# Delta-rule attention: operands of 128 columns for the products with the state and with the solved values

## The chip, the cores and the metric

The kernel runs on one core of one Trainium2 chip. The core has five engines that run side by side, each with its own row of instructions in a fixed order: TensorE (PE, the matrix products), VectorE (DVE), ScalarE (ACT), GpSimd (POOL) and SyncE (SP, which here only issues DMAs). They wait for each other by semaphores. TensorE writes its products into PSUM, which this program cuts into eight banks of 512 fp32 numbers for each of the 128 partitions; DVE and ACT read them there. The metric is the device time of one execution in microseconds (us).

## The reference

Two stages run one after the other: a delta-rule attention over 768 tokens (4 batches, 8 heads, head size 48), and a feed-forward net with a squared ReLU over the 3072 rows that come out of it.

```python
def _attn_ref(q, k, v, beta):
    B, H, S, D = q.shape                                   # 4, 8, 768, 48
    k_n = k / (np.linalg.norm(k, axis=-1, keepdims=True) + 1e-06)
    state = np.zeros((B, H, D, D), dtype=np.float32)
    y = np.zeros_like(q)
    for t in range(S):
        kt, vt, bt = (k_n[:, :, t], v[:, :, t], beta[:, :, t, None])
        y[:, :, t] = np.einsum('bhd,bhde->bhe', q[:, :, t], state)
        v_old = np.einsum('bhde,bhd->bhe', state, kt)
        state = state + bt[:, :, :, None] * np.einsum('bhd,bhe->bhde', kt, vt - v_old)
    return y

def _moe_ref(x, w_in, w_out):                              # (3072, 384), (384, 2048), (2048, 384)
    h = np.maximum(x @ w_in, 0.0)
    return h * h @ w_out
```

## The kernel before

**Chunks.** The tokens are cut into 12 units of 64 (`units`, `C`). Within a unit the recurrence is solved as a triangular system: with the scores of keys against keys masked below the diagonal, the values corrected by what the state at the unit's start already holds (keys times state) are multiplied by the inverse of that system (`solved`, L549); then the state gets keys times solved values, and the output is queries times old state plus masked query-key scores times solved values. All 32 pairs of batch and head of a unit are treated together: 64 tokens lie on half of the 128 partitions, batches b and b + 2 side by side as `c`, the heads as four pairs p of an even and an odd one (j).

**Steps of a unit.**
- `load`, `load_q`: keys go by DMA into one of three tiles `kpad`, queries into `qpad`, each head padded from 48 to 64 columns with zeros that L90 and L93 have put there at the program's start. `normalize` (L285 to L298) divides the keys by their norms.
- `static`: keys and queries are transposed on TensorE, one head pair per instruction (L335), copied from PSUM by ACT (L338, tile `kq`), multiplied to key-key and key-query scores (L351), which DVE masks (L361, tile `ap`). The first two units do this in two halves, keys first and queries later, with copies on ACT and the mask on POOL. The key-key scores go out to DRAM and come back in another layout (`lt`).
- `invert`: DVE inverts diagonal blocks of 32 x 32 column by column (L448, L449; for the first two units together L446 and L449). The result goes through DRAM into `tt`.
- `whole`: the off-diagonal blocks by two sets of 32 x 32 products (L490, L500; DVE transposes one operand, L483; ACT copies the result to `tt`, L506). Between them stand the products with the old state, two sets of 64 x 48 outputs (L525): keys first, into two banks of pool x, which DVE subtracts from the values (L533), then queries, into two banks of pool g, where they stay.
- `solved`, then `onward`: keys times solved values (L565) into two x banks, which DVE adds to `state`; masked scores times solved values (L574) on top of what stands in the g banks; ACT copies the sum out as `y` (L578).
- `moe` of the unit: y is transposed (L591) and split into a high and a low fp32r part, and the two products with the weights run as three terms each (L625 into an h bank, Relu, Square and split on ACT and DVE at L632 to L635 and L604, and L612 into the o banks).

The feed-forward weights are split at the start and during unit 1 in the same manner (L138 to L163).

**PSUM.** Pools g, x, h and o have two banks each. Tiles of a pool are given out in turn: who wants a bank waits until its last reader is done.

**What sets the order.** Each engine's order is written out by hand: the program lists pieces of work (generators), and `weave` merges them by places between 0 and 1 in a unit. `CHAIN` gives the four places of `whole` (two parts), `solved` and `onward` among 32 steps of the feed-forward of the unit before. While the state part of unit u runs, the feed-forward of unit u - 1 fills TensorE.

Of the kernel before, what the change touches and what calls it, by code (L numbers as in the profile page):

```python
# [21 lines left out]
def kernel(  # L22
# [42 lines left out]
    ps_x = ctx.enter_context(tc.tile_pool(name="ps_x", bufs=2, space=bass.MemoryType.PSUM))  # L65
# [15 lines left out]
    mask = const.tile([P, 2, C], F32, name="mask")  # L81
    nc.gpsimd.memset(mask, 1.0)
    for b in range(2):
        half = mask[b * C:(b + 1) * C, 1]
        nc.gpsimd.affine_select(out=half, in_=half, pattern=[[1, C]], base=0, channel_multiplier=-1,
                                compare_op=ALU.is_gt, fill=0.0)
    kpad = []
    for i in range(3):
        kp = const.tile([P, NC, H, C], F32, name=f"kpad{i}")
        nc.gpsimd.memset(kp[:, :, :, D:], 0.0)  # L90
        kpad.append(kp)
    qp = const.tile([P, NC, H, C], F32, name="qpad")
    nc.gpsimd.memset(qp[:, :, :, D:], 0.0)  # L93
# [132 lines left out]
    def split_bank():  # L226

        turn[1] += 1
        return (ps_o.tile([P, PC], F32, name=f"o{turn[1] % 2}") if split_early else ps_x.tile([P, PC], F32, name="x"))
# [7 lines left out]
    def load_to(dst, x, d, width, queues=None):  # L237
# [6 lines left out]
        for j, queue in enumerate(queues or (nc.sync, nc.sync)):  # L244
            for b, src in enumerate(tokens(x, d)):
                rows = slice((b ^ j) * C, (b ^ j) * C + C)
                for c in range(NC):
                    queue.dma_start(out=dst[rows, c, j::2, :width], in_=src[:, c, j::2])

    def load(u):  # L250
        d = dict(u=u, y=[None] * NC)
        d["kp"] = kpad[u % 3]
        load_to(d["kp"], k, d, D, (nc.sync, nc.scalar) if u <= 1 else None)
        return d

    def load_q(d):

        d["qp"] = kpad[2] if d["u"] == 1 else qp
        load_to(d["qp"], q, d, D)
# [13 lines left out]
    def load_v(d):  # L273
        d["vt"] = apool.tile([P, NC, H, D], F32, name="vt", bufs=2)
        load_to(d["vt"], v, d, D)

    def normalize(d):

        n2, s0, s1 = [apool.tile([P, H2], F32, name=f"{n}{d['u'] % 2}", bufs=1) for n in ("n2", "s0", "s1")]
        kn = d["kp"].rearrange("p c h d -> p (c h) d")[:, :, :D]  # L280
        squares = []
        for c in range(NC):
            sq = (apool.tile([P, H, D], F32, name="r", bufs=2) if d["u"] in (2, 3) else
                  spool.tile([P, PC], F32, name="rest")[:, :H * D].rearrange("p (h e) -> p h e", h=H))
            nc.scalar.activation(out=sq, in_=kn[:, c * H:(c + 1) * H], func=AF.Square)  # L285
            squares.append(sq)
        yield
        for c, sq in enumerate(squares):
            nc.vector.tensor_reduce(out=n2[:, c * H:(c + 1) * H], in_=sq, axis=AX.X, op=ALU.add)  # L289
# [11 lines left out]
        nc.vector.tensor_tensor(out=kn, in0=kn, in1=s1.unsqueeze(2).broadcast_to(list(kn.shape)), op=ALU.mult)  # L301
        yield

    def x_tile(u=2):

        turn[0] += 1
        pool, name = (ps_h, "h") if u <= 1 and turn[0] % 4 >= 2 else (ps_x, "x")
        return pool.tile([P, PC], F32, name=name)


    def static(d):

        u = d["u"]
        room = dram.tile([4, H2, HB, HB], F32, name="blocks")

        kq = apool.tile([P, NC, NP, 2, 2, C], F32, name="kq", bufs=2)
        ap = apool.tile([P, NC, H, 2, C], F32, name="ap", bufs=2)
        d["kq"], d["ap"] = kq, ap


        def banks(c):
            if c == 0 or u <= 1:
                return [x_tile(u) for _ in range(2)]
            g = ps_g.tile([P, 2, PC], F32, name="g")
            return [g[:, 0], g[:, 1]]

        def transposed(parts, pair, into):

            pair = [x.rearrange("p (x n t) -> p x n t", x=2, n=NP) for x in pair]
            for x, (c, which) in enumerate(parts):  # L330
                src = d["qp" if which else "kp"]
                for p in range(NP):
                    for b in range(2):
                        rows = slice(b * C, (b + 1) * C)
                        nc.tensor.transpose(pair[b][:, x, p], src[rows, c, 2 * p:2 * p + 2].rearrange("p a b -> p (a b)"),  # L335
                                            ident[rows, rows])
            for b in range(2):
                nc.scalar.copy(out=into[:, :, :, b], in_=pair[b])  # L338

        def products(c, first, n):  # L340

            ps = [x[:, :NP * n * C].rearrange("p (n t) -> p n t", n=NP) for x in banks(c)]
            for p in range(NP):
                for j in range(2):
                    rows = slice(j * C, j * C + D)
                    for x in range(first, first + n) if j else (first,):
                        for b in range(2):

                            to = b if x or not j else 1 - b
                            m = 1 if j else n  # L350
                            nc.tensor.matmul(ps[j][to * C:(to + 1) * C, p, (x - first) * C:(x - first + m) * C],  # L351
                                             lhsT=kq[rows, c, p, b, 0],
                                             rhs=kq[rows, c, p, b, x:x + m].rearrange("p x t -> p (x t)"),
# [3 lines left out]
        def heads(c, j):  # L357
            return ap[:, c].rearrange("p (n j) x t -> p j n x t", j=2)[:, j]

        def masked(c, j, ps):  # L360
            nc.vector.tensor_tensor(out=heads(c, j).rearrange("p n x t -> p n (x t)"), in0=ps,  # L361
                                    in1=mask.rearrange("p x t -> p (x t)").unsqueeze(1).broadcast_to([P, NP, 2 * C]),
# [463 lines left out]
```

## Time and profile before

| | |
|---|---|
| runs | 637.03, 636.20, 636.87 us; median 636.87 |
| the profiled execution | 636.73 us, of which the span below is 635.0 |
| mean granted TensorE clock | 0.969 |
| L612, the second feed-forward product | 333.7 us busy (203.8 with `h_h`, 129.9 with `h_l`) |
| L625, the first one | 268.4 us busy (168.9 with `x_h`, 99.5 with `x_l`) |
| DMA | 49.91 MB, mean 79 GB/s |

Matmuls overlap each other, so busy times of PE lines add up to more than PE's own.

```profile
DVE  4699757786595694793894884874875964841211
ACT  4733578545454445445536446444454535355442
PEclk9965699999999999999999999999999999999999
```

Each digit is the busy share of a slice of 15.9 us, in tenths. DVE is half to nine tenths busy until the last units, ACT about half, and the clock granted to TensorE (last line) is below nine tenths only in slices three to five, at the start, where the weights are split.

### The profile page before, as it was taken

How to read it: one execution, taken by the hardware profiler on the slowest of the kernel's cores; microseconds unless marked ns; L12 is line 12 of the kernel's file. 1: busy time of each engine (PE TensorE's matmuls, PEld its weight loads, DVE VectorE, ACT ScalarE, POOL GpSimd, SP SyncE). 2: the span in 40 equal slices, each digit the busy share in tenths (PEclk: the TensorE clock that was granted, in tenths of full speed). 3: DMA queues.
4: the chain of work that ended last, by engine and by line, in shares of the span. 5: the costliest groups of instructions: out<-in, count | busy, mean ns of one | idle time of the engine just before them, and what ended most of it. 6: DMA issues, size and time to landing. Idle time of an engine off the chain costs nothing.

```text
span 635.0 us, 22958 instructions
## 1 busy us (share of the span) xinstructions
PE 585.2 (92%) x9908; PEld 548.3 (86%) x9908; DVE 409.9 (65%) x1121; ACT 316.2 (50%) x620; POOL 35.6 (6%) x61
## 2 busy tenths in 40 slices
PE   2950799889999999999999999999999999999997
PEld 1540469889999999999999999999999999999996
DVE  4699757786595694793894884874875964841211
ACT  4733578545454445445536446444454535355442
POOL 5021100001001001001001000010010010000000
PEclk9965699999999999999999999999999999999999
DMA  7785955213524526317217226236235144030101
GB/s 222 198 208 145 222 139 106 40 26 59 88 52 71 85 43 108 65 27 122 56 32 121 54 40 114 54 47 101 53 52 94 28 63 83 2 68 3 26 0 26
DMA packets 173724, 49.91 MB, mean 79 GB/s; under 512 B 165424, under 2 KB 168504, under 8 KB 173624
## 3 DMA queue, kind: packets, MB, share of 16 engines
q1 hardware_dynamic: 170072, 47.72, 38.4%
q8 instruction: 78, 1.28, 0.9%
q10 hardware_dynamic: 3424, 0.72, 0.6%
q14 instruction: 22, 0.18, 0.1%
q0 software_dynamic: 128, 0.01, 0.0%
HBM read 37.32 MB, written 11.01 MB: 76 GB/s over the span
## 4 chain that ended last, share of the span: by engine, by line
PE 86%; DVE 8%; DMA 2%; ACT 1%; issue 1%; SPq 1%; DVEq 0%
PE o L612 33%; PE h L625 32%; PE o L163 2%; PE x L351 2%; DVE h_h L446 2%; DVE tt L449 2%; PE g L525 2%; PE x L525 2%; PE x L549 2%; PE x L565 2%; PE g L574 2%; PE g L351 2%; PE h L490 1%; PE x L500 1%; PE h L591 1%
## 5 line engine op out<-in xcount | busy, mean ns | idle before, releaser
L612 PE MATMUL o<-w,h_h 128*128 128x384 f32 x768 | 203.8, 347 | 0.0
L604 DVE TENSOR_TENSOR h_l<-r,h_h 128x512 fp32r<-128x512 f32 x96 | 67.8, 707 | 164.0 <-PE o L612 127.0
L625 PE MATMUL h<-x_h,w 128*128 128x256 f32 x1152 | 168.9, 282 | 0.7 <-issue 0.4
L632 ACT ACTIVATE r<-h 128x512 f32<-128x512 f32 x96 | 57.5, 598 | 207.0 <-PE h L625 206.9
L625 PEld LDWEIGHTS h<-x_h,w 128*128 128x128 f32 x1152 | 154.0, 189 | 1.9 <-issue 0.6
L612 PEld LDWEIGHTS o<-w,h_h 128*128 128x128 f32 x768 | 133.8, 188 | 3.1
L612 PE MATMUL o<-w,h_l 128*128 128x384 f32 x384 | 129.9, 338 | 0.0
L448 DVE SCALAR_TENSOR_TENSOR tmp<-lt,bt,z 128x126 f32<-128x126 f32 (+22 forms) x310 | 95.6, 308 | 7.5
L625 PE MATMUL h<-x_l,w 128*128 128x256 f32 x576 | 99.5, 282 | 0.0
L449 DVE TENSOR_TENSOR z<-z,tmp 128x126 f32<-128x126 f32 (+22 forms) x310 | 79.2, 255 | 10.6
L625 PEld LDWEIGHTS h<-x_l,w 128*128 128x128 f32 x576 | 81.6, 189 | 0.0
L612 PEld LDWEIGHTS o<-w,h_l 128*128 128x128 f32 x384 | 72.3, 188 | 0.0
L633 ACT ACTIVATE r<-r 128x512 f32<-128x512 f32 x96 | 60.7, 632 | 3.0
L635 ACT CAST h_h<-r 128x512 fp32r<-128x512 f32 x96 | 59.5, 620 | 3.1
L432 POOL MEMSET z<- 128x512 f32 x10 | 5.3, 526 | 434.6 <-DMA inv<-z 346.3
L490 PEld LDWEIGHTS h<-tt,ap 32*32 32x32 f32 x768 | 8.2, 109 | 22.5 <-ACT w L156 19.2
L490 PE MATMUL h<-tt,ap 32*32 32x32 f32 x768 | 9.6, 198 | 19.4 <-DMA tt<-inv 19.4
L291 ACT ACTIVATE s<-n 128x16 f32<-128x16 f32 x12 | 2.6, 216 | 39.9 <-DVE n L289 31.8
L351 PE MATMUL x<-kq 48*64 48x64 f32 (+1 forms) x608 | 20.4, 256 | 1.4 <-ACT kq L338 1.3
L351 PEld LDWEIGHTS x<-kq 48*64 48x64 f32 x608 | 17.9, 152 | 3.4 <-ACT kq L338 2.1
L335 PE MATMUL x<-plus,kpad 64*128 64x64 f32 x104 | 7.7, 245 | 11.8 <-DMA w<-in_moe_w_in_dram 11.8
L506 ACT ACTIVATE tt<-x 32x256 f32<-32x256 f32 x44 | 16.4, 373 | 0.6
(121 smaller groups left out, 669.7 us busy)
## 6 DMA issues: line engine op xcount, KB each, us to landing
w<-in_moe_w_in_dram SPq DMA_DIRECT2D x12, 512.0 KB
w<-in_moe_w_out_dram SPq DMA_DIRECT2D x16, 384.0 KB
lt<-blocks SPq DMA_DIRECT2D x22, 256.0 KB
vt<-in_v_dram SPq DMA_DIRECT2D x48, 96.0 KB
out_dram<-a SPq DMA_DIRECT2D x46, 96.0 KB
kpad<-in_k_dram SPq DMA_DIRECT2D x88, 48.0 KB
qpad<-in_q_dram SPq DMA_DIRECT2D x88, 48.0 KB
blocks<-ap SPq DMA_DIRECT2D x48, 64.0 KB
```

Source lines behind the costliest of these rows:

```text
L351: nc.tensor.matmul(ps[j][to * C:(to + 1) * C, p, (x - first) * C:(x - first + m) * C], lhsT=kq[rows, c, p, b, 0], rhs=kq[rows, c, p, b, x: ...
L448: nc.vector.scalar_tensor_tensor(out=tmp, scalar=bt[:, s:s + 1], op0=ALU.mult, op1=ALU.mult, **factors)
L449: nc.vector.tensor_tensor(out=z[:, :nj, s + 1:], in0=z[:, :nj, s + 1:], in1=tmp, op=ALU.subtract)
L490: nc.tensor.matmul(ps[at[h % 2][b], h // 2], lhsT=ap[lower[b], c, e, 0, :HB], rhs=tt[lower[b], c, e, HB:], start=True, stop=True)
L506: nc.scalar.mul(out=right[upper[b], j, :, HB:], in_=ps[j][upper[b]], mul=-1.0)
L525: nc.tensor.matmul(dst[j][to, c, p], lhsT=d["kq"][rows, c, p, b, x], rhs=state[rows, b, c, p], start=(c == 0 and p == 0) if x else True, s ...
L604: nc.vector.tensor_tensor(out=h_l, in0=r, in1=h_h.bitcast(F32), op=ALU.subtract)
L612: nc.tensor.matmul(o[i], lhsT=a[:, e, i * P:(i + 1) * P], rhs=halves["wo", ft][w], start=(ft == 0 and n == 0), stop=(ft == FT - 1 and n == 2))
L625: nc.tensor.matmul(hp[:, e], lhsT=halves["wi", (kt, ft // EACH)][w][:, f], rhs=x[:, kt], start=(n == 0), stop=(n == 3 * KT - 1))
L632: nc.scalar.activation(out=r, in_=hp, func=AF.Relu)
L633: nc.scalar.activation(out=r, in_=r, func=AF.Square)
L635: nc.scalar.copy(out=h_h, in_=r)
```

## The change

**One tile of four parts.** `kpad` and `qpad` become three tiles `kx`, which hold for each head pair four places of 64 columns: even key, odd query, even query, odd key (`3 * j` for keys, `2 - j` for queries). Two of them are cleared whole at the start, the third only in its padding. The masked scores of a pair later overwrite the two query places, so that keys and masked scores lie side by side.

**Operands of 128 columns.** Keys and queries on the state become one set of products, with key and query of a head side by side as the stationary operand (`on_state`, L526); so do keys and masked scores on the solved values (`onward`, L562). A product fills all 128 partitions of its bank, one half for the state or the values and the other for the output. Each set has 32 matmuls, where two sets of 32 stood. Four matmuls of one column (L555) go ahead of `onward`'s set; nothing reads what they write.

**PSUM.** Pool x goes; g is one tile of four banks, h and o stay at two. The transposes and the scores of `static`, the products on the state with L501 behind them, and the sums with solved values take the g tile in turn; `solved`, the scores of the first two units and the weight split beside unit 1, which had x banks (the first two partly h), now take h banks.

**Reading it.** Half of a bank holds what one reader wants, so four instructions of 64 partitions stand where two of 128 stood: the subtraction from the values (L532) and the copies of y (L573). The state is added in two of 64 partitions and 768 elements (L569). In `static` ACT copies the key-key scores (L407) and DVE masks only the others (L408). The copies of `kq` (L330) are two of 1024 elements instead of four of 512. The third place of `CHAIN`, of `solved`, moves from 21.9 to 22.5. `normalize` puts the squares of units 2 and 3 into another tile.

The lines shown come from both files; "..." leaves out.

```diff
-    kpad = []
     for i in range(3):
-        kp = const.tile([P, NC, H, C], F32, name=f"kpad{i}")
-        nc.gpsimd.memset(kp[:, :, :, D:], 0.0)
-    qp = const.tile([P, NC, H, C], F32, name="qpad")
-    nc.gpsimd.memset(qp[:, :, :, D:], 0.0)
+        kx = const.tile([P, NC, NP, 4, C], F32, name=f"kx{i}")
+        nc.gpsimd.memset(kx[:, :, :, :, D:] if i == 2 else kx, 0.0)
...
-                    queue.dma_start(out=dst[rows, c, j::2, :width], in_=src[:, c, j::2])
+                    queue.dma_start(out=dst[rows, c, :, 2 - j if x is q else 3 * j, :D], in_=src[:, c, j::2])
...
+    def g_tile():
+        return ps_g.tile([P, 4, PC], F32, name="g")
...
-        def heads(c, j):
-            return ap[:, c].rearrange("p (n j) x t -> p j n x t", j=2)[:, j]
+        def plain(c, j):
+            return ap[:, c].rearrange("p (n j) t -> p j n t", j=2)[:, j]
+        def masked(c, j):
+            return kx[:, c, :, 1 + j]
...
-        for c in range(NC):
-            transposed([(c, 0), (c, 1)], banks(c), kq[:, c].rearrange("p n b x t -> p x n b t"))
-        yield
-        for c, pair in enumerate([products(c, 0, 2) for c in range(NC)]):
+        transposed(*[(slice(0, P), slice(c, c + 1), slice(0, 2)) for c in range(NC)])
+        yield
+        g = g_tile()
+        for c, pair in enumerate([products(c, 0, 2, [g[:, 2 * c + j] for j in range(2)]) for c in range(NC)]):
             for j, ps in enumerate(pair):
-                masked(c, j, ps)
+                ps = ps.rearrange("p n (x t) -> p n x t", x=2)
+                nc.scalar.copy(out=plain(c, j), in_=ps[:, :, 0])
+                nc.vector.tensor_tensor(out=masked(c, j), in0=ps[:, :, 1],
+                                        in1=mask.unsqueeze(1).broadcast_to([P, NP, C]), op=ALU.mult)
...
+        d["g"] = g_tile()
         if u:
-            keys_on_state(d)
+            on_state(d)
         yield
-        ps = [x_tile(u)[:, :H * HB].rearrange("p (k t) -> p k t", k=H) for _ in range(2)]
+        ps = [[d["g"][upper[j], 2 * j + b, :H * HB].rearrange("p (k t) -> p k t", k=H) for b in range(2)] for j in range(2)]
...
-        if u:
-            queries_on_state(d)
...
+    def on_state(d):
+        g = areas([d["g"][:, x] for x in range(4)])
         for c in range(NC):
             for p in range(NP):
                 for j in range(2):
                     rows = slice(j * C, j * C + D)
                     for b in range(2):
-                        to = slice((b ^ j) * C, ((b ^ j) + 1) * C)
-                        nc.tensor.matmul(dst[j][to, c, p], lhsT=d["kq"][rows, c, p, b, x], rhs=state[rows, b, c, p],
+                        nc.tensor.matmul(g[2 * j + b][:, c * NP + p], lhsT=d["kq"][rows, c, b, p].rearrange("p x t -> p (x t)"),
+                                         rhs=state[rows, b, c, p], start=(c == 0 and p == 0), stop=False,
...
+        for j in range(2):
+            for b in range(2):
+                left = by_parity(d["vt"][HALF[b ^ j]])[:, j]
+                nc.vector.tensor_tensor(out=left, in0=left, in1=g[2 * j + b][HALF[j]], op=ALU.subtract)
...
-        tv = areas([x_tile(u) for _ in range(2)], NP)
+        tv = areas([h_tile() for _ in range(2)])
...
-                        nc.tensor.matmul(ku[b][j * C:(j + 1) * C, c, p], lhsT=kp[rows, c, h], rhs=uu[rows, c, h],
...
-                    nc.tensor.matmul(gy[j][to, c, p], lhsT=ap[rows, c, h, 1], rhs=uu[rows, c, h],
...
+                    nc.tensor.matmul(out[2 * j + b][:, c * NP + p],
+                                     lhsT=kx[HALF[b], c, p, 2 * j:2 * j + 2].rearrange("p x t -> p (x t)"),
+                                     rhs=uu[HALF[b], c, h], start=(u == 0 and c == 0 and p == 0), stop=True,
...
+                nc.vector.tensor_tensor(out=now, in0=now, in1=g[HALF[j], 2 * j:2 * j + 2, :NC * NP * D], op=ALU.add)
+        d["y"] = y = apool.tile([P, NC, H, D], F32, name="y", bufs=1)
+        for j in range(2):
+            for b in range(2):
+                nc.scalar.copy(out=by_parity(y[HALF[b ^ j]])[:, j], in_=out[2 * j + b][HALF[1 - j]])
...
-    CHAIN = (14.9, 18.4, 21.9, 25.4)
+    CHAIN = (14.9, 18.4, 22.5, 25.4)
```

**On TensorE, at the state products of unit 3.** Here is the row before, from the end of the first 32 x 32 set (L490) through the keys on the state; o_2886 and o_2887 are the two o banks, w_... the weights, and a word in brackets is a semaphore that the instruction waits for, named by the engine or DMA queue that raises it.

```order
L490 MATMUL h<-tt_110,ap 32x32 [waits DMAHW6_49]
L490 MATMUL h<-tt_110,ap 32x32 x30
L525 MATMUL x<-state,kq 64x48 x32
L612 MATMUL o_2886<-w_413,h_h 128x384 x2
L612 MATMUL o_2886<-w_413,h_l 128x384
```

And the same unit before, 27 rows further on, at the second 32 x 32 set with the queries on the state behind it.

```order
L612 MATMUL o_2887<-w_829,h_l 128x384
L500 MATMUL x<-m,t_3121 32x32 [waits DVE_49,PE_49,Activation_49]
L500 MATMUL x<-m,t_3121 32x32
L500 MATMUL x<-m,t_3121 32x32 [waits DVE_49,PE_49]
L500 MATMUL x<-m,t_3121 32x32 x29
L525 MATMUL g<-state,kq 64x48 x32
L612 MATMUL o_2886<-w_836,h_h 128x384 x2
```

These are the two places in the changed kernel; there the state products write all of g, and L501 writes into g as well.

```order
L490 MATMUL h<-tt_105,ap 32x32 [waits DMAHW6_49]
L490 MATMUL h<-tt_105,ap 32x32 x30
L526 MATMUL g<-state,kq 128x48 x32
L605 MATMUL o_2762<-w_434,h_h 128x384 x2
L605 MATMUL o_2762<-w_434,h_l 128x384
```

The second of them, again 27 rows on:

```order
L605 MATMUL o_2763<-w_876,h_l 128x384
L501 MATMUL g<-m,t_2999 32x32 [waits DVE_49,Activation_49]
L501 MATMUL g<-m,t_2999 32x32 x31
L605 MATMUL o_2762<-w_883,h_h 128x384 x2
L605 MATMUL o_2762<-w_883,h_l 128x384
```

The queries' set has gone from behind the second 32 x 32 set into the first place, and the waits of L501 stand on its first instruction alone.

**On VectorE, between those two places.** Before, in unit 3: n_3090 takes the squares' sums of the keys two units ahead, t_3121 is L483's result for L500.

```order
L604 TENSOR_TENSOR h_l<-r,h_h 128x512 [waits DVE_49,PE_49,Activation_49] x2
L289 TENSOR_REDUCE n_3090<-rest 128x8 x2
L483 STREAM_TRANSPOSE t_3121<-t1t 128x256 [waits DMAHW2_49,DMAHW7_49,DMAHW1_49,DMAHW0_49]
L533 TENSOR_TENSOR vt<-vt,x 128x8x48 x2
L448 SCALAR_TENSOR_TENSOR tmp<-lt,bt,z 128x31 [waits DMAHW5_49,DMAHW4_49,DMAHW6_49,DMAHW3_49,Pool_49]
```

And in the changed kernel, the same place of unit 3:

```order
L597 TENSOR_TENSOR h_l<-r,h_h 128x512 [waits DVE_49,PE_49,Activation_49] x2
L286 TENSOR_REDUCE n_2968<-rest 128x8 x2
L483 STREAM_TRANSPOSE t_2999<-t1t 128x256 [waits DMAHW2_49,DMAHW7_49,DMAHW1_49,DMAHW0_49]
L532 TENSOR_TENSOR vt<-vt,g 64x8x48 x4
L448 SCALAR_TENSOR_TENSOR tmp<-lt,bt,z 128x31 [waits DMAHW5_49,DMAHW4_49,DMAHW6_49,DMAHW3_49,Pool_49]
```

Nothing has changed places; the two subtractions have become four of half the partitions.

**On ScalarE, at the transposes and scores of unit 4, in the row of unit 3.** Before, kq is copied from an x and a g pair, and the next Relu (L632) follows; the scores are DVE's.

```order
L594 CAST x_h<-h 128x6x64 [waits PE_49] x2
L338 COPY kq<-x 128x2x4x64 [waits PE_49] x2
L338 COPY kq<-g 128x2x4x64 [waits PE_49]
L338 COPY kq<-g 128x2x4x64
L632 ACTIVATE r<-h 128x512 [waits DVE_49,PE_49]
```

In the changed kernel, the copies of the key-key scores stand ahead of the next Relu (L625).

```order
L587 CAST x_h<-h 128x6x64 [waits PE_49] x2
L330 COPY kq<-g 128x1024 [waits PE_49]
L330 COPY kq<-g 128x1024
L407 COPY ap<-g 128x4x64 [waits PE_49]
L407 COPY ap<-g 128x4x64 [waits DVE_49] x3
L625 ACTIVATE r<-h 128x512 [waits PE_49]
```

Four copies have become two, and four more have been added, three of which wait for DVE.

More of the change, by code (lines that the diff above doesn't have):

```diff
@@ L300, in normalize, with h_tile @@
         yield
-        nc.vector.tensor_tensor(out=kn, in0=kn, in1=s1.unsqueeze(2).broadcast_to(list(kn.shape)), op=ALU.mult)
+        nc.vector.tensor_tensor(out=kn, in0=kn, in1=s1.rearrange("p (n j) -> p n j", j=2).unsqueeze(3).broadcast_to(list(kn.shape)),
+                                op=ALU.mult)
         yield
[L304 to L308, printed above, removed]
+    def h_tile():
+        return ps_h.tile([P, PC], F32, name="h")
@@ L327, in transposed @@
[L327 to L338, printed above, removed]
@@ L340, in products, with transposed @@
-        def products(c, first, n):
-            ps = [x[:, :NP * n * C].rearrange("p (n t) -> p n t", n=NP) for x in banks(c)]
+        def transposed(*places):
+            g = g_tile()
+            for c in range(NC):
+                for x in range(2):
+                    for p in range(NP):
+                        for b in range(2):
+                            rows = slice(b * C, (b + 1) * C)
+                            nc.tensor.transpose(g[:, 2 * c + b, (2 * p + x) * C:(2 * p + x + 1) * C],
+                                                kx[rows, c, p, 2 * x:2 * x + 2].rearrange("p x t -> p (x t)"), ident[rows, rows])
+            for rows, c, x in places:
+                to = kq[rows, c].rearrange("p c b n x t -> p (c b n) x t")[:, :, x]
+                nc.scalar.copy(out=to, in_=g[rows, 2 * c.start:2 * c.stop].rearrange("p g (n x t) -> p (g n) x t", n=NP, x=2)[:, :, x])
@@ L343, in products @@
+        def products(c, first, n, ps):
+            ps = [x.rearrange("p (n t) -> p n t", n=NP) for x in ps]
             for p in range(NP):
@@ L390, in static @@
             yield
-            transposed([(c, 1) for c in range(NC)], [x_tile(u) for _ in range(2)], kq[:, :, :, :, 1])
+            transposed(*[(rows[1 - x], every, x) for x in range(2)])
             yield
+            pair = [h_tile() for _ in range(2)]
             for c in range(NC):
-                for j, ps in enumerate(products(c, 1, 1)):
-                    nc.scalar.copy(out=heads(c, j)[:, :, 1], in_=ps)
+                part = slice(c * NP * C, (c + 1) * NP * C)
+                for j, ps in enumerate(products(c, 1, 1, [x[:, part] for x in pair])):
+                    nc.scalar.copy(out=masked(c, j), in_=ps)
             yield
@@ L499, in whole @@
                 rows = at[h % 2][b]
[L500 to L502 removed]
+                nc.tensor.matmul(ps[h % 2][b][:, h // 2], lhsT=t1[rows, h // 2], rhs=m[rows, h // 2], start=True, stop=True)
         right = tt.rearrange("p c (k j) t -> p j (c k) t", j=2)
```

144 lines of the change are left out of this document (61 added, 83 removed).

## Prediction

> **What bounds the kernel now.** I read the page from the top (busy shares, slices), then the chain that ended last, then one steady iteration as a timeline.
>
> ```profile
> span 635.0 us, 22958 instructions
> ...
> PE 585.2 (92%) x9908; PEld 548.3 (86%) x9908; DVE 409.9 (65%) x1121; ACT 316.2 (50%) x620; POOL 35.6 (6%) x61
> ...
> PE   2950799889999999999999999999999999999997
> ...
> PE o L612 33%; PE h L625 32%; PE o L163 2%; PE x L351 2%; DVE h_h L446 2%; DVE tt L449 2%; PE g L525 2%; PE x L525 2%; PE x L549 2%; PE x L565 2%; PE g L574 2%; PE g L351 2%; PE h L490 1%; PE x L500 1%; PE h L591 1%
> ...
> 184.50:230.00 45.50, 45.50 (x830) 43.90 (x830) 31.78 (x93) 22.38 (x44) 2.42 (x3) 1.00 0.41 69
> ```
>
> The profiled execution took 636.73 us (its span and 1.7 around it); the median of the runs shown is 636.87, so sums on the one hold for the other. There are two regimes. From the seventh slice on PE has no gap: in the iteration from 184.5 to 230.0 (the columns are length, then busy PE, PEld, DVE, ACT, POOL) PE is busy all 45.5 us. There, PE time saved is saved and each new PE wait is paid. In the first six slices PE is mostly idle and a chain over k, DVE's inversion and the weight split decides.
>
> **The products on PE.** An fp32 matmul is two passes in the trace, each with its own weight load.
>
> ```profile
> 252.51 1.15 PE L525 MATMUL x<-state,kq 48*64 48x48 f32 x64
> 253.59 0.62 PE L612 MATMUL o<-w,h_h 128*128 128x384 f32 x2
> ...
> 258.04 0.84 PE L500 MATMUL x<-m,t 32*32 32x32 f32 x64
> 258.81 1.15 PE L525 MATMUL g<-state,kq 48*64 48x48 f32 x64
> 259.89 0.62 PE L612 MATMUL o<-w,h_h 128*128 128x384 f32 x2
> ...
> 263.27 1.15 PE L549 MATMUL x<-vt,tt 64*64 64x48 f32 x64
> ...
> 268.78 1.15 PE L565 MATMUL x<-vt,kpad 64*64 64x48 f32 x64
> ...
> 269.75 1.11 PE L574 MATMUL g<-vt,ap 64*64 64x48 f32 x64
> ...
> 270.79 0.62 PE L612 MATMUL o<-w,h_h 128*128 128x384 f32 x2
> ```
>
> Start to next start, 64 passes of 64 columns take 0.97 where the same shape follows (L565) and 1.08 where the array goes back to 128x128 (L525): 15.2 ns a pass and 0.11 to leave. One unit's products cost 1.08 + 1.08 (keys, queries on state) and 0.97 + 1.04 (keys and masked scores on solved values): 4.17. Afterwards each pair is 64 passes instead of 128, with 128 columns each. The trace has that stationary operand, 64 rows by 128 columns, in the transposes:
>
> ```profile
> 232.34 0.42 PE L335 MATMUL x<-plus,kpad 64*128 64x64 f32 x8
> 232.60 0.41 PE L335 MATMUL x<-plus,qpad 64*128 64x64 f32 x8
> 232.84 0.41 PE L335 MATMUL g<-plus,kpad 64*128 64x64 f32 x8
> ```
>
> Eight passes per 0.25 us: 62.5 ns for a pair (one in each half of the rows), 31 a pass, twice the 15.2 of a 64-column pass. So the count halves and the price doubles. Bounds: as dear as now per pass, 15.2; nearest row, 31, which I take, as the shape is the same.
>
> The Trainium skill, "TensorE: Matmul & The Clock Gate", section "LDWEIGHTS (loading the stationary operand)", says that a load's time goes with its columns, P/1.2 ns, whatever the rows. The trace agrees with the proportion, not the size (62.5 against the page's 107 for 128 columns); at 107 for each of the 736 pairs the products would cost 33 us more than in my sum, by an estimate from that page.
>
> State products: 32 x 0.0625 + 0.11 = 2.11 for 2.16, units 1 to 11: -0.5. Onward: four dummy matmuls are eight 64-column passes, 0.12, and one more change of array shape, 0.11; then 2.11. That is 2.34 for 2.01 in units 1 to 10: +3.3; unit 0 has no dummies, +0.1; the last unit did only the L574 half (1.04) and now does all, +1.3. **Together +4.2**; at 15.2 a pass the sum is -19.6.
>
> **A wait of PE for DVE.** The keys on state used to lie in x banks, subtracted by two DVE instructions; now they fill one half of the rows of all four g banks, four instructions of 64 partitions subtract them, and L501 writes its products into the same g rows, so its first matmul waits for the fourth. DVE at that place:
>
> ```profile
> 255.00 0.69 DVE L604 TENSOR_TENSOR h_l<-r,h_h 128x512 fp32r<-128x512 f32 x1 [5.52 <-PE o L612]
> 255.61 1.01 DVE L289 TENSOR_REDUCE n<-rest 128x8 f32<-128x384 f32 x2
> 256.53 0.44 DVE L483 STREAM_TRANSPOSE t<-t1t 128x256 f32<-128x256 f32 x1
> 256.89 0.98 DVE L533 TENSOR_TENSOR vt<-vt,x 128x384 f32<-128x384 f32 x2
> ...
> L533 DVE TENSOR_TENSOR vt<-vt,x 128x384 f32<-128x384 f32 x22 | 10.8, 528 | 0.0
> ```
>
> DVE is held at L604 until the six L612 after the state products end (255.00, 1.41 after 253.59); nothing behind it can start earlier. L533 follows at 256.89 and ends at 257.87, with PE reaching L500 at 258.04: in time by a hair. Elements are as many per partition, so four take 0.53 + 3 x 0.45 = 1.88 and end at 258.77; with a hand-over of 0.04, L501 starts 0.77 late. Behind it PE's whole row of feed-forward matmuls waits. Units 2 to 9: 8 x 0.77 = **+6.2**. Units 10 and 11 have no L289 (no key is normalised any more), 1.0 earlier: nothing. In unit 1 the weight split lies between: nothing. Bounds 4 to 8.
>
> **ACT and DVE take turns on one g tile.** Products used to be evacuated by four L361 on DVE alone. Now four ACT copies (L407) and four DVE products (L408) alternate, each waiting for the other, behind the last of PE's products; and the Relu that frees an h bank stands behind the last copy on ACT.
>
> ```profile
> 239.93 1.10 PE L351 MATMUL g<-kq 48*64 48x64 f32 x46
> ...
> 242.34 0.60 ACT L632 ACTIVATE r<-h 128x512 f32<-128x512 f32 x1 [6.97 <-PE h L625]
> ...
> 244.28 0.87 PE L625 MATMUL h<-x_h,w 128*128 128x256 f32 x6
> ...
> L385 ACT COPY ap<-h 128x256 f32<-128x256 f32 x4 | 1.5, 375 | 0.3 <-PE x L351 0.2
> ...
> L361 DVE TENSOR_TENSOR ap<-x,mask 128x512 f32<-128x512 f32 x20 | 12.9, 686 | 1.7 <-PE x L351 0.6
> ```
>
> A 128x256 copy is 375 ns (L385); the DVE product is 0.37 (686 at 512 elements, 528 at 384, 158 less for each 128). From 241.07 four copies, three products and six hand-overs of 0.04 end at 243.92; Relu 0.60 ends at 244.52, where PE asks for the bank at 244.28: +0.3 an iteration, ten times, **+3**. Bounds 0 (the hand-overs overlap) to 6. The h ring also serves the solved values now, but CHAIN 22.5 puts six L612 (1.06) between the last h matmul and them, longer than the Relu of 0.60, and six more before the next h: I cost it at nothing; without that cover, 0.6 in eleven units.
>
> DVE's other extras (state sums 64x768, some 0.8 more a unit) fall into its waits for PE. L330's copies are not late: products come 5.5 us after the transposes. The y copies of ACT (four for two) come 5 us before they are asked for.
>
> **The start.** kx0 and kx1 are cleared whole (2048 elements), and the first k load, at the head of the SP and ACT queues, waits for that.
>
> ```profile
> 1.08 0.56 POOL L90 MEMSET kpad<- 128x256 f32 x2
> ...
> 6.99 1.01 POOL L432 MEMSET tt<- 128x1024 f32 x1
> ...
> 0.80 5.83 SPq L248 DMA_DIRECT2D kpad<-in_k_dram  x8
> ...
> 6.45 0.94 ACT L285 ACTIVATE rest<-kpad 128x384 f32<-128x384 f32 x2 [2.98 <-DMA kpad<-in_k_dram]
> ...
> 11.78 0.34 PE L335 MATMUL x<-plus,kpad 64*128 64x64 f32 x1 [11.78 <-DMA w<-in_moe_w_in_dram]
> ...
> 12.96 0.59 ACT L338 COPY kq<-x 128x512 f32<-128x512 f32 x1
> ...
> 20.30 2.43 PE o L163 x3
> ...
> 24.07 0.36 DVE L146 TENSOR_SCALAR r<-w 128x384 int32<-128x384 int32 x1 [4.11 <-ACT w L138]
> ...
> 30.96 1.22 DVE L439 TENSOR_TENSOR lt<-lt,bt 128x1024 f32<-128x1024 f32 x1
> ...
> 84.36 0.98 PE g L574 x62
> ...
> 85.36 0.87 ACT y L578 x2
> ...
> 86.44 0.37 DVE a L146
> ```
>
> Twice 1.01 for 2048 elements: SP starts at 3.0 instead of 0.80, 2.2 late; ACT also stops for the identity, made after both clears: 3. Then each of the first two units transposes 32 operands for 16 (107 ns a pair at the clock granted there, 0.5: 0.9), copies 1024 elements twice for 512 twice (0.9 more), and its second half of products waits until ACT has emptied the first, in the same two banks (0.7): 2.5 a unit. Part of this may go into waits that exist (DVE's 4.11 at 24.07). All of it stands ahead of L163 at 20.30, which feeds the split, which stands on DVE ahead of L439; the inversion follows without a gap. **+8**, bounds 2 and 11. At the end of unit 0, y left g as soon as L574 was done; now it waits for both state sums (2.0) and is four copies (1.6 for 0.87), with the split's ACT and DVE work behind it: **+2.5**, bounds 0 and 3.
>
> **Sum**: 4.2 + 6.2 + 3 + 8 + 2.5 = 23.9, so 636.73 + 23.9 = 660.6; I say 660.
>
> **The rivals.**
> Not slower: a pass costs by the instruction, not by its columns. Place: the 736 pairs of L526 and L562. The products then give -19.6, and the rest, 19.7, eats it: 637. It decides below 30 ns a pair, where the transposes show 62.5; for it speaks only that those are another operation with a longer moving operand (64 for 48). 0.08, of which 0.05 below 636.
> The Trainium skill, "TensorEngine Tiling (Array Packing)", section "Instruction Overhead", gives each matmul some 60 cycles of overhead, which would favour half as many instructions. The trace, at 15.2 ns a pass with quarters in turn, shows no such floor.
> Row halves don't overlap: L526 issues four passes on one half before the other. At 62.5 each, 4.1 for 2.11 in eleven units, +22: 682. Against it: L525 has that order already and takes 1.15 like L549, which alternates. 0.07.
> The start is hidden: its 8 goes into the wait at 24.07 and what follows: 652. 0.12.
> The h ring stalls: solved values wait for the Relu in spite of CHAIN, 0.6 to 1 in eleven units: 669. For it: ACT is late by the third term. 0.09.
> That it doesn't halve the products is out: the instructions do halve; only the work in each doubles.
>
> **The numbers.** Forecast 0.64, range 648 to 670 from the bounds that are likely together. The range 646 to 672 adds the hidden start and the h ring and leaves out the row halves and the first rival, some 0.17. A measurement can tell about 0.2% from no change: faster 0.05, within 0.03, slower 0.92.
>
> **What would show it.** L526 and L562 at 2.0 to 2.1 us a group (1.1 would make the first rival true). L501 named in PE's waits for DVE L532, some 0.8 in units 2 to 9 and nothing in the last two. L618 waiting for ACT L625 some 0.3 after the products. L439 starting near 39 and the first gap-free PE iteration some 10 later. It is wrong if L439 starts before 33, or if PE's iterations of 45.4 do not grow to about 46.8.

## The result, and the profile after

The changed kernel takes 722.91 us, the median of four runs from 719.36 to 727.25, beside 636.95: 1.135 times as long, 95% interval 1.128 to 1.142. Slower was right; 660, and the range to 672, were far too low. The profiled execution took 720.87 us, 84.1 more than the one before.

The page after, in the lines that answer to those of before (busy times, slices of TensorE and of its clock, chain by lines):

```profile
span 719.1 us, 20449 instructions
...
PE 650.5 (90%) x8652; PEld 609.5 (85%) x8652; DVE 427.4 (59%) x1143; ACT 347.3 (48%) x664; POOL 38.8 (5%) x60
...
PE   1860788989999999999999999999999999999997
...
PEclk9965798999999989899999999999999999999999
...
PE o L605 25%; PE h L618 18%; PE g L562 6%; PE g L526 3%; PE g L344 3%; DMA kx<-in_q_dram 3%; DVE vt L532 2%; PE o L162 2%; SPq L241 2%; ACT ap L407 2%; PE g L326 2%; SPq L467 2%; DVE kx L408 2%; DVE h_h L446 2%; DVE tt L449 2%
```

TensorE has 1256 matmul records less and is busy 65 us more, and the clock line has eights where only nines stood. The timeline of TensorE shows why (start, length, line, shapes, count). First at the state products of unit 4:

```profile
288.70 0.75 PE L490 MATMUL h<-tt,ap 32*32 32x32 f32 x64
289.38 4.79 PE L526 MATMUL g<-state,kq 48*128 48x48 f32 x64
294.11 1.01 PE L605 MATMUL o<-w,h_h 128*128 128x384 f32 x2
294.91 0.52 PE L605 MATMUL o<-w,h_l 128*128 128x384 f32 x1
```

Then in unit 5:

```profile
341.74 3.81 PE L526 MATMUL g<-state,kq 48*128 48x48 f32 x64
345.48 0.62 PE L605 MATMUL o<-w,h_h 128*128 128x384 f32 x2
...
349.63 0.34 PE L605 MATMUL o<-w,h_l 128*128 128x384 f32 x1
351.14 0.74 PE L501 MATMUL g<-m,t 32*32 32x32 f32 x64 [1.17 <-DVE vt L532]
```

And the sums with solved values behind the next ones, with the wait of L618 for the Relu that recurs in each unit:

```profile
281.04 0.99 PE L618 MATMUL h<-x_h,w 128*128 128x256 f32 x6 [0.17 <-ACT r L625]
...
360.73 0.29 PE L555 MATMUL g<-kx 64*64 64x1 f32 x8
360.95 3.78 PE L562 MATMUL g<-vt,kx 64*128 64x48 f32 x64
364.66 0.62 PE L605 MATMUL o<-w,h_h 128*128 128x384 f32 x2
```

A set of 64 passes takes 3.74 us from start to next start (unit 5) where 2.11 was forecast; L562 takes 3.70. In unit 4 the state products take 4.73, and the L605 behind it lie 0.32 apart (294.91 to the next at 295.23) instead of 0.18: the clock has halved in the middle of the set. The windows give the granted clock as the third figure from the end:

```profile
288.70:293.90 5.20, 5.20 (x129) 5.16 (x128) 0.00 (x0) 1.26 (x3) 0.00 (x0) 0.82 1.06 165
293.90:299.00 5.10, 5.10 (x23) 5.01 (x23) 2.50 (x6) 0.21 (x1) 0.00 (x0) 0.52 0.37 65
```

TensorE is busy in all of both windows. The trace's clock has nine such stretches at 0.5 between the start and the last products, each 3.41 or 6.83 us long; in the profile before there were none (in the runs with blocks behind that kernel, two of three had one of 3.41 us, at 137 us). The seven from unit 2 on each begin 2.6 to 4.2 us after the start of a 128-column set. The two ahead of them, in units 0 and 1, have no such set in the 5 us before them: TensorE had just waited 2.98 and 1.27 us there, ahead of L162, the weight split.

Where the 84.1 us lie (rounded), by the starts of the transposes of y (L591 before, L584 after), which open each unit's feed-forward:

| | before | after | more |
|---|---|---|---|
| to the first one (unit 0) | 93.1 | 106.4 | 13.3 |
| unit 1 | 48.0 | 57.6 | 9.5 |
| units 2 to 10, together | 409.3 | 464.3 | 55.0 |
| the rest | 84.6 | 90.9 | 6.3 |

An iteration without a stretch takes 50.4 to 50.6 for 45.4: 3.49 from the sets (3.74 + 3.70 + 0.22 for the four L555, against 4.17), 1.24 ahead of L501 (by starts; idle time 1.17), 0.40 among the L618 behind L344. Nine times 5.13 is 46.2; the other 8.8 is what the six stretches there add, net: three of those units have little or no wait ahead of L501, and one iteration before was 0.8 longer than the rest.

### The profile page after: what moved, and what is told of

The parts are those of the page before. It is cut to its first block, busy times and chain, and to the rows that moved or that the text cites. A ratio compares the mean times of both kernels' runs of the same rounds, so it can differ in the third digit from the quotient of the medians.

```text
span 719.1 us, 20449 instructions
## 1 busy us (share of the span) xinstructions
PE 650.5 (90%) x8652; PEld 609.5 (85%) x8652; DVE 427.4 (59%) x1143; ACT 347.3 (48%) x664; POOL 38.8 (5%) x60
## 4 chain that ended last, share of the span: by engine, by line
PE 64%; DVE 12%; SPq 10%; ACT 5%; DMA 5%; issue 3%; POOL 1%; DVEq 0%; ACTq 0%; POOLq 0%
PE o L605 25%; PE h L618 18%; PE g L562 6%; PE g L526 3%; PE g L344 3%; DMA kx<-in_q_dram 3%; DVE vt L532 2%; PE o L162 2%; SPq L241 2%; ACT ap L407 2%; PE g L326 2%; SPq L467 2%; DVE kx L408 2%; DVE h_h L446 2%; DVE tt L449 2%
## 5 line engine op out<-in xcount | busy, mean ns | idle before, releaser
L605 PE MATMUL o<-w,h_h 128*128 128x384 f32 x768 | 210.5, 356 | 0.0
L618 PE MATMUL h<-x_h,w 128*128 128x256 f32 x1152 | 173.7, 287 | 3.2 <-ACT r L625 3.0
L618 PEld LDWEIGHTS h<-x_h,w 128*128 128x128 f32 x1152 | 158.3, 194 | 6.4 <-ACT r L625 5.3
L605 PEld LDWEIGHTS o<-w,h_h 128*128 128x128 f32 x768 | 137.9, 195 | 4.0 <-DVE a L640 0.7
L605 PE MATMUL o<-w,h_l 128*128 128x384 f32 x384 | 133.3, 347 | 0.0
L625 ACT ACTIVATE r<-h 128x512 f32<-128x512 f32 x96 | 57.4, 598 | 107.7 <-PE h L618 107.5
L618 PE MATMUL h<-x_l,w 128*128 128x256 f32 x576 | 100.8, 284 | 0.0
L618 PEld LDWEIGHTS h<-x_l,w 128*128 128x128 f32 x576 | 83.3, 192 | 0.0
L605 PEld LDWEIGHTS o<-w,h_l 128*128 128x128 f32 x384 | 74.9, 195 | 0.2
L407 ACT COPY ap<-g 128x256 f32<-128x256 f32 x40 | 14.9, 372 | 67.0 <-PE g L344 51.2
L562 PE MATMUL g<-vt,kx 64*128 64x48 f32 x768 | 46.8, 278 | 0.0
L573 ACT COPY y<-g 64x384 f32<-64x384 f32 x48 | 22.7, 474 | 49.5 <-DVE state L569 47.1
L562 PEld LDWEIGHTS g<-vt,kx 64*128 64x128 f32 x768 | 45.2, 193 | 0.5 <-issue 0.4
L526 PE MATMUL g<-state,kq 48*128 48x48 f32 x704 | 42.9, 277 | 0.0
L526 PEld LDWEIGHTS g<-state,kq 48*128 48x128 f32 x704 | 41.5, 191 | 0.5
L326 PE MATMUL g<-plus,kx 64*128 64x64 f32 x448 | 19.2, 246 | 15.7 <-DMA w<-in_moe_w_in_dram 14.2
```

The costliest lines, as they stand in the source:

```text
L326: nc.tensor.transpose(g[:, 2 * c + b, (2 * p + x) * C:(2 * p + x + 1) * C], kx[rows, c, p, 2 * x:2 * x + 2].rearrange("p x t -> p (x t)"), ...
L407: nc.scalar.copy(out=plain(c, j), in_=ps[:, :, 0])
L526: nc.tensor.matmul(g[2 * j + b][:, c * NP + p], lhsT=d["kq"][rows, c, b, p].rearrange("p x t -> p (x t)"), rhs=state[rows, b, c, p], start ...
L562: nc.tensor.matmul(out[2 * j + b][:, c * NP + p], lhsT=kx[HALF[b], c, p, 2 * j:2 * j + 2].rearrange("p x t -> p (x t)"), rhs=uu[HALF[b], c ...
L605: nc.tensor.matmul(o[i], lhsT=a[:, e, i * P:(i + 1) * P], rhs=halves["wo", ft][w], start=(ft == 0 and n == 0), stop=(ft == FT - 1 and n == 2))
L618: nc.tensor.matmul(hp[:, e], lhsT=halves["wi", (kt, ft // EACH)][w][:, f], rhs=x[:, kt], start=(n == 0), stop=(n == 3 * KT - 1))
```

## The experiments

**What a pass costs, by itself.** Blocks of 32 matmuls behind the last product of the kernel before; they differ in the row and column halves (r, c) that they use, in stationary columns and in moving columns.

```diff
+        both, quarters = [(0, 0), (1, 0)], [(0, 0), (1, 1), (0, 1), (1, 0)]
+        block(both, P, 48)
+        block([(0, 0)], P, 48)
+        block(both, P, 24)
+        block(both, P, 96)
+        block(both, P, 64, True)
+        block([(0, 0)], P, 64, True)
+        block(quarters, C, 48)
+        block([(0, 0), (0, 1)], C, 48)
+        block(both, C, 48)
+        block([(0, 0)], C, 48)
...
+        block(both, P, 64, single=True)
+        block([(0, 0)], P, 64, single=True)
```

> The kernel before, unchanged, with blocks of 32 fp32 matmuls (64 passes) behind its last product, each block apart from the next by copies on ACT; nothing reads their results. In the changed kernel a pass with 128 columns on half the rows cost 55.7 ns. Theory A (passes on the two row halves follow each other, passes on the two column halves run side by side, and a pass lasts by its weight load): 128 columns cost 56 ns a pass whether the halves alternate or not and whether 24, 48 or 96 columns move; 64 columns cost 28 to 30 with one column half, alternating rows or not, and 15 with both column halves. Theory B (halves would overlap, but the two passes of one fp32 matmul stand on the same half, so that the order is at fault): alternating halves is cheaper than one half alone, and single-pass matmuls that alternate cost about 31 a pass against 56 on one half. Theory C (the moving columns set it): 24 moving columns cost about half of 48, 96 twice as much. The transposes, alternating, should show 31 a pass as in the kernel; on one half 31 by C, 56 to 62 by B.

TensorE's timeline of that kernel, a row per block in this order; L811 are transposes, L813 single-pass fp32r matmuls:

```profile
631.50 3.77 PE L815 MATMUL g<-kpad,kpad 64*128 64x48 f32 x64
639.42 13.88 PE L815 MATMUL g<-kpad,kpad 64*128 64x48 f32 x64 [4.15 <-ACT rest L820]
655.47 7.02 PE L815 MATMUL g<-kpad,kpad 64*128 64x24 f32 x64 [2.17 <-ACT rest L820]
...
677.36 1.97 PE L811 MATMUL g<-plus,kpad 64*128 64x64 f32 x32 [6.07 <-ACT rest L820]
684.11 3.67 PE L811 MATMUL g<-plus,kpad 64*128 64x64 f32 x32 [4.78 <-ACT rest L820]
690.27 1.96 PE L815 MATMUL g<-kpad,kpad 64*64 64x48 f32 x64 [2.48 <-ACT rest L820]
700.53 3.65 PE L815 MATMUL g<-kpad,kpad 64*64 64x48 f32 x64 [8.31 <-ACT rest L820]
708.37 3.65 PE L815 MATMUL g<-kpad,kpad 64*64 64x48 f32 x64 [4.19 <-ACT rest L820]
716.09 7.06 PE L815 MATMUL g<-kpad,kpad 64*64 64x48 f32 x64 [4.07 <-ACT rest L820]
...
748.57 3.62 PE L813 MATMUL g<-minus,plus 64*128 64x64 f32 x32 [12.15 <-ACT rest L820]
756.98 7.03 PE L813 MATMUL g<-minus,plus 64*128 64x64 f32 x32 [4.78 <-ACT rest L820]
```

The first block ran at clock 1.0, the others shown here at 0.5. From start to start, a 128-column pass takes 56 ns at clock 1.0 where both row halves alternate, and at 0.5 it takes 107 with 24 moving columns; on one row half it takes 214 at 0.5. A 64-column pass takes 107 on one quarter at 0.5, 54 on two, whether they share rows or columns, and 26.5 on four. At clock 1.0 the blocks of the experiment on the clock, further down, give 55.6 and 113 for 128 columns (both halves, one half), 29.2 for two quarters and 14.7 for four. So all three theories fall. Halves do overlap, rows as well as columns; a pass lasts by its stationary columns, not by its moving ones (55.8 with 64 of them, 56.0 with 96, at clock 1.0); and the quarters of the array work at the same time. A 128-column operand costs what two 64-column ones cost that follow each other on one quarter, and gives away what the quarters had. **A transpose's pass takes half of that**: 108 ns on one half and 55 alternating, at clock 0.5, where a single-pass matmul with an operand of the same shape takes 214 and 107.

The Trainium skill, "TensorE: Matmul & The Clock Gate", section "LDWEIGHTS (loading the stationary operand)", gives P/1.2 ns, 107 for 128 columns. The matmuls come near it (113 at clock 1.0 on one row half; at 0.5 twice the 107), the transposes don't; the prediction had believed the transposes.

**The changed kernel with operands of 64 columns.** Every 128-column matmul becomes two, nothing else changes; the first run does it in both places, the second in `on_state` alone, and the third adds a start that clears in parts.

```diff
-                    nc.tensor.matmul(out[2 * j + b][:, c * NP + p],
-                                     lhsT=kx[HALF[b], c, p, 2 * j:2 * j + 2].rearrange("p x t -> p (x t)"),
+                    for x in range(2):
+                        nc.tensor.matmul(out[2 * j + b][HALF[x], c * NP + p], lhsT=kx[HALF[b], c, p, 2 * j + x],
...
-        nc.gpsimd.memset(kx[:, :, :, :, D:] if i == 2 else kx, 0.0)
+        nc.gpsimd.memset(kx[:, :, :, :, D:], 0.0)
+        if i < 2:
+            nc.vector.memset(kx[:, :, :, 1:3, :D], 0.0)
```

> The changed kernel with its operands cut back to 64 columns (each 128-column matmul as two, keys and queries, keys and masked scores), everything else as changed. If the 128-column passes are what costs, and the half-speed stretches of TensorE's clock follow from them: the two sets fall from 3.74 and 3.70 to about 2.1 and 2.0 us, the nine stretches at clock 0.5 are gone, and the time is 661 (656 to 666), near my forecast. Rival, the stretches have another cause (PSUM turns, a denser PE): sets fall the same, stretches stay, 675 or more. Rival, the PSUM layout with its waits is what costs: above 690.

> The changed kernel with the state products alone cut back to 64 columns; keys and masked scores on solved values stay at 128. If each 128-column set costs 1.6 us and brings its own share of half-speed stretches: 11 x 1.6 = 18 and about half of the 17 us that the stretches take, so 696 (690 to 703), four or five stretches. If stretches come only when two sets per unit stand close: none left, 688.

> As the run with 64 columns, and the first two kx tiles cleared in parts: the padding on POOL, the query places on DVE, so that the first loads of keys wait for nothing. If the start's 8 us came from the loads and the identity behind the clears: 2 to 3 us earlier at the first transpose, and 3 to 5 in all, 657. If it came from the transposes, copies and scores of the first two units: under 1 us.

Measured: 683.19 (1.0715, 1.069 to 1.074), 705.2 (1.106, 1.103 to 1.108) and 683.43 (1.071, 1.068 to 1.074). With 64 columns the sets are back at 2.05 and 1.99 us, and 40 of the 86 us go; each of the two places with 128-column sets costs some 20 in all (22.0 for `onward`, 17.7 for `on_state`). But 683 isn't 661: five stretches at 0.5 remain. Three of them follow places where L527 itself stands still, with more work ready, as here in unit 5:

```profile
326.14 1.71 PE L527 MATMUL g<-state,kq 48*64 48x48 f32 x98
330.37 0.84 PE L527 MATMUL g<-state,kq 48*64 48x48 f32 x30 [2.52 <-issue]
331.15 1.01 PE L606 MATMUL o<-w,h_h 128*128 128x384 f32 x2
```

"issue" says that it waits for nothing that the profile shows; a transfer of 16 KB of instructions starts at 327.46. So this run tells the price of the sets, not the cause of the stretches. The second run lies above its 690 to 703 too: it has seven stretches for the four or five expected, and L527 stands still in it twice. The partial clears bring the first transpose from 14.2 to 11.6 us and L490 of unit 0 (L492 there) from 75.1 to 72.3, so the loads and the identity are 2 to 3 us of the start, as expected. Unit 0's end, 105.1 and 100.5 in these two profiles, tells less: the second has a half-speed stretch less there and a shorter one at the start, and a later run with the same clears has 104.0. The medians are the same, not 3 to 5 us apart; single runs spread over 680 to 685.

**What halves the clock.** A row of matmuls without a wait behind the kernel before, dense stretches between the blocks (here the first of two such kernels; the second has other blocks in these places):

```diff
+        dense(60)
+        block(both, P, 48, 90)
+        dense(60)
+        block(both, P, 96, 90)
...
+        for _ in range(6):
+            block(both, P, 48, 16)
+            dense(6)
```

> The kernel before, with an unbroken row of matmuls behind its last product: stretches of 60 dense fp32r matmuls (128x128, 384 columns, about 10.6 us) and between them (1) 180 passes of 128 columns on alternating row halves with 48 moving columns, 10 us; (2) the same with 96 moving columns; (3) 64 columns on one column half, alternating rows, 360 passes; (4) 64 columns on all four quarters, 640 passes; (5) six times 32 passes as in (1) with six dense ones behind each. No engine waits. Theory L (the clock goes to 0.5 after a stretch of 3.4 us in which the array streams little, though PE never waits): (1) and (3), which stream 48 columns in 56 and 27 ns a pass, fall to 0.5 within 3.4 to 6.8 us; (2) and (4) stream twice as much and show from where on it holds; (5) keeps 1.0. Theory I (only idle PE lowers the clock): all keep 1.0. Theory P (128-column passes as such): (1), (2) and (5) fall, (3) and (4) don't.

> As the run on the clock, with other stretches between the dense ones: (1) 128 columns on alternating halves, 64 moving columns, (2) the same with 80, (3) 64 columns on one column half, alternating rows, 24 moving, (4) 64 columns on one row half, both column halves, 48 moving, (5) 128 columns on one half alone, 96 moving. If what counts is how many moving columns the array takes in a microsecond (860 lowered the clock, 1690 did not): (3) with 24 per 27 ns = 890 and (5) with 96 per 107 ns = 900 fall, (4) with 48 per 27 ns keeps, and (1) at 1150 and (2) at 1430 show where between. If it counts by the width of the operand, (3) keeps and (1), (2), (5) fall.

Windows of the first of these kernels (blocks 1, 2, 3, 4 and the broken one; the clock is third from the end):

```profile
642.60:658.60 16.00, 16.00 (x181) 15.98 (x180) 0.00 (x0) 0.00 (x0) 0.00 (x0) 0.61 0.01 2
...
671.40:681.50 10.10, 10.10 (x181) 10.08 (x180) 0.00 (x0) 0.00 (x0) 0.00 (x0) 1.00 0.01 3
692.30:702.80 10.50, 10.50 (x360) 10.49 (x360) 0.00 (x0) 0.00 (x0) 0.00 (x0) 1.00 0.02 5
713.50:728.20 14.70, 10.05 (x641) 9.68 (x640) 0.00 (x0) 0.00 (x0) 0.00 (x0) 1.00 0.02 4
738.90:756.60 17.70, 17.70 (x223) 16.15 (x222) 0.00 (x0) 0.00 (x0) 0.00 (x0) 1.00 0.01 2
```

And of the second (1 to 5):

```profile
640.90:651.00 10.10, 10.10 (x181) 10.08 (x180) 0.00 (x0) 0.00 (x0) 0.00 (x0) 1.00 0.01 3
661.70:671.80 10.10, 10.10 (x181) 10.10 (x180) 0.00 (x0) 0.00 (x0) 0.00 (x0) 1.00 0.01 3
682.60:696.70 14.10, 14.10 (x360) 14.10 (x360) 0.00 (x0) 0.00 (x0) 0.00 (x0) 0.72 0.01 3
709.95:720.50 10.55, 10.55 (x361) 10.54 (x360) 0.00 (x0) 0.00 (x0) 0.00 (x0) 1.00 0.01 3
731.20:747.00 15.80, 15.80 (x97) 15.71 (x96) 0.00 (x0) 0.00 (x0) 0.00 (x0) 0.67 0.00 1
```

A TensorE that is busy without a gap loses half its clock where it streams, at clock 1.0, 48 moving columns per 55.6 ns (860 a us), 24 per 29.2 (820) or 96 per 113 (850), with wide operands and narrow ones alike, and keeps it with 64 per 55.8 (1150) and with more. So Theory L holds in these ten blocks, each executed once, and I and P fall; the first expectation was wrong on its block 3, whose 48 columns come every 29.2 ns, twice as often. Broken up by six dense matmuls after each 32 passes, the same passes keep the clock. The Trainium skill, "TensorE: Matmul & The Clock Gate", section "What's actually happening", tells of a free-running window of 3413 ns whose busy-ness sets the clock; the stretches of 3.41 and 6.83 us agree, and so does it that a set of 3.74 us brings one in some units only.

**The sets cut in two, 2.1 us of feed-forward between the halves.** `on_state` and `onward` yield between c = 0 and c = 1.

```diff
+            if c:
+                yield
...
-    CHAIN = (14.9, 18.4, 22.5, 25.4)
+    CHAIN = (14.9, 16.9, 19.4, 22.5, 25.4, 27.4)
```

> The changed kernel with each 128-column set cut in two halves of 32 passes, two steps of feed-forward products (2.1 us) between them, and the second 32 x 32 set one step later. The passes stay at 56 ns (a set 3.6 + 0.1 to 0.2). If the half-speed stretches come from sets that fill a window of 3.4 us: none or one left after unit 0, 16 us less, some given back where VectorE and ScalarE are late: 709 (703 to 714), and a smaller spread between runs. If they come from the total of such passes or from something else: as many stretches, 722 or more.

> The same two halves with operands of 64 columns. Sets at 2.05 + 0.2 and 2.0 + 0.2, no place where L527 stands still for 2.6 us (three in the run with 64 columns, each with a transfer of instructions), no half-speed stretch after unit 1: 683 - 8 - 10 = 665 (660 to 670). If the stretches of that run had another cause than the standstills and the sets: 675 or more.

Measured: 710.01 (1.114, 1.110 to 1.117) and 681.58 (1.070, 1.068 to 1.072). With 128 columns a half set takes 1.92 to 1.95, two stretches remain behind unit 1 (seven before) where none or one was expected, and the time falls by 13, within its range: the window account has it so. With 64 columns stretches and standstills are gone from unit 2 on, and yet it is 17 more than expected: the iteration is an even 48.4, for the cut itself brings new waits. L589, the transposes of y, waits for the copies of y ("PE h L589 <- ACT y L578: 5.5, 9, 0.6" in its list of waits), and there are more changes of shape. So its miss tells of the cut in the main, not of the change.

**The queries on the state behind the second 32 x 32 set, as before.**

```diff
-            on_state(d)
+            on_state(d, 0)
...
+        if u:
+            on_state(d, 1)
```

> 64 columns, the start with partial clears, and the queries on the state behind the second 32 x 32 set again, as before; what stays of the change is the PSUM layout, the evacuation by ScalarE and VectorE in turn, the copies by half partitions and the kx tile. If my accounts of the rest hold: no standstill and no half-speed stretch after unit 1, the wait ahead of L503 at 0.2 for 1.2, an iteration of 46.2 against 45.4 before; 683 - 4.6 (start) - 8 (standstills) - 8 (stretches) - 8 (wait) = 655 (651 to 659). Rival: the layout itself brings the stretches, 665 or more.

Measured: 696.25 (1.090, 1.083 to 1.097), 41 more than expected. Each of the two sets takes 2.03 us, not 1.08: 21 of the 41. In the new layout a head's parity fixes both its row half and its place in the operand, so that the keys alone use two quarters of the array on a diagonal: 64 passes at 29.9 ns, near the 29.2 of the blocks with two quarters. Only both together fill four. Before, the batch chose the column half, and each set alone had all four. The other 20 come with what the expectation had put away: the wait ahead of L503 is still 1.17 in most units, and there are six stretches, four of which begin in the set behind that wait. So this run doesn't settle its rival, that the layout itself brings the stretches.

**State products one step later, with 64 columns and with 128.** `on_state` stands six feed-forward products (L605 in the changed kernel) behind L490, L501 one step later, the start is cleared in parts.

```diff
         if u:
+            yield
             on_state(d)
...
-    CHAIN = (14.9, 18.4, 22.5, 25.4)
+    CHAIN = (14.9, 15.9, 19.4, 22.5, 25.4)
```

> 64 columns, partial clears at the start, the state products one step behind L492 and the second 32 x 32 set one step later. If the wait for VectorE, the standstills and the stretches are what made the run with 64 columns longer than its sums, they go together: an iteration of 46.0 (45.4 and 0.4 for the Relu, 0.1 to 0.2 for one more change of shape), unit 0 done at 100.5, 650 in all (645 to 655). If stretches or standstills stay without a wait, the layout brings them in another way: 660 or more.

> The same kernel with the operands of 128 columns as changed: the price of the operands alone, in one pair. 11 x 1.7 + 12 x 1.7 = 39 for the passes, and 5 to 15 for half-speed stretches, since each set still fills a window of 3.4 us: 44 to 54 over its partner, 694 to 704 if that is at 650.

Measured: 665.99 (1.042, 1.039 to 1.046) and 717.77 (1.126, 1.122 to 1.130). The pair, equal in all but the operands, differs by 51.8, within what was expected: that is what the operands of 128 columns cost here, some 39 in the passes of their 23 sets and the rest with the stretches that they bring (twelve, for five with 64). With 64 columns the quiet iteration is 46.0 to the tenth, and the wait ahead of L504 is gone, as expected; but standstills ("PE g L530 <- issue: 4.3, 4, 1.3" among its waits) and stretches stay, two of them behind such standstills, so the time lies where the expectation had put its rival, at 660 or more. The 28.5 that it is still over the kernel before are not the operands: of the 32.8 in the profiled execution, 11.0 lie ahead of unit 0's end, 6.9 in unit 1 and 13.7 in units 2 to 10. What brings the standstills, and the stretches in units 0 and 1, stays open.

None of these beats the kernel before.

## Why the prediction was wrong, point by point

- **The products on PE**, forecast +4.2: by starts, the three lines take 90.5 us (L526 42.1, L562 45.9, L555 2.4) for 47.1 before, +43.3, 2.4 of it because four sets ran partly at half clock. This is the step that failed: "62.5 ns for a pair ..., which I take, as the shape is the same". The shape was the same, the operation wasn't: a transpose's pass takes half of a matmul's. A pair costs 111.2 to 112.3 in the two sets, and 736 pairs at 49 more are 36 of the 39 that were missing. And where it read 15.2 ns a pass with "quarters in turn", four quarters work at once, which a 128-column operand gives up.
- **The clock** was no term at all. I held the granted clock of before for a given. A 128-column set lasts longer than a stretch of 3.41 us and streams 860 columns a us: the stretches come to a net 8.8 us in units 2 to 10 of this profile. The spread of 8 us between runs goes with the clock: 0.945 on average in the two faster ones, 0.935 and 0.934 in the others.
- **The wait for DVE**, forecast +6.2: 7.9 us idle in eight waits. In units 2 to 9 it is 7.2: 1.14 to 1.17 in six of them, 0.2 in unit 9, none in unit 4, where PE came late from a stretch; unit 10 has none. Unit 1, where nothing was forecast, has 0.72. Mechanism and place were right. DVE was held to 1.41 after the set as before; the four L532 take 2.21 rather than 1.88.
- **ACT and DVE in turn**, forecast +3 (its rows give 0.24 each): 0.40 in each of nine iterations from unit 2 on, 3.6.
- **The start**, forecast +8: L490 of unit 0 begins at 75.0 for 66.5, +8.5, and L439 at 39.3, as forecast. The clears are 2.6 of it (first transpose 14.2 to 11.6 without them); the other 6 weren't taken apart.
- **The end of unit 0**, forecast +2.5: 4.8, of which 1.7 are L562's price; the rest, 3.1, is near the forecast, and L162 waits 2.98 for ACT (L164) there, so the cause fits.
- **Unit 1**, not forecast as a whole: 9.5. The sets are 3.3 of it, and a stretch of 6.83 us lies in it, up to 3.4, which is not behind one of the sets. The weight split and the feed-forward share the h ring there, which the prediction did not price (its cover of six L612 is that of the solved values); L618 and L162 wait 1.50 and 1.27 us for the Relu in that unit. The prediction saw no gap of PE from the seventh slice on, but its digits for the next two are eights: that is unit 1, with waits of 1.6 and 2.1 before the change too. A run of its own for this wasn't tried, and its share stays open.
- **The rivals.** "Row halves don't overlap" named nearly the right price, 4.1 a set for 3.74, and the wrong cause: they do overlap. The 107 ns for 128 columns of the Trainium skill, "TensorE: Matmul & The Clock Gate", section "LDWEIGHTS (loading the stationary operand)", which the prediction priced at 33 us more and set aside, was the better figure: a pair measured 111 to 112.

## What to carry to other kernels

Price a matmul's pass from a matmul with an operand of the same shape, not from a transpose, and count how many parts of the array hold loads at the same time: half as many instructions with twice the columns can leave the array's parts idle. Then ask how many columns stream in each microsecond; a stretch of passes that stream little, as long as the 3.41 us of the clock's stretches here, slows what stands behind it too. Such stretches can be broken up with dense work, as the cut sets show, if the cut doesn't bring waits of its own.

## What the runs showed of the hardware that was not expected

- A TensorE busy without a gap fell to clock 0.5 in the blocks with 820 to 860 moving columns a us, 3.6 to 6.2 us after their start, and kept 1.0 at 1150 or more; between the two nothing was tried. Dense work then needed 3.0 to 5.5 us to get the clock back.
- At clock 0.5, a transpose's pass with 128 columns on one row half takes 108 ns, that of a matmul, of one pass or two, 214.
- A run of small matmuls may outpace the supply of instructions. In the block with four quarters 273 passes went through at 15 ns, and then each 128 were followed by a standstill. Transfers of 16 KB of instructions land at 717.82 and 721.62, each 1.4 us before TensorE goes on; that they are the cause is argued from this order alone:

```profile
713.45 4.22 PE L814 MATMUL g<-kpad,kpad 64*64 64x48 f32 x273
719.26 2.08 PE L814 MATMUL g<-kpad,kpad 64*64 64x48 f32 x128 [1.59 <-issue]
723.00 2.08 PE L814 MATMUL g<-kpad,kpad 64*64 64x48 f32 x128 [1.67 <-issue]
```
